# Weight decodes from buffers of their own, spread between the attention steps of a Nystrom attention and MoE kernel

## The chip, the cores and the metric

The kernel runs on one core of a Trainium2 chip. The metric is the device time of one execution in microseconds (us), taken as the median of several runs. The engines are PE (TensorE, matrix products), DVE (VectorE), ACT (ScalarE), POOL (GpSimd) and SP (SyncE, which issues most DMAs here).

## What is computed

The inputs are random q, k, v (4 batches, 8 heads, 576 positions, 64 wide, float32) and weights that arrive as float64.

```python
# attention, per batch and head (32 landmarks: means of 18 rows each)
A, Bm, C = sm(q, k_lm), sm(q_lm, k_lm), sm(q_lm, k)      # softmax of scaled products
Z = Bm.T / (norm1(Bm) * norminf(Bm) + 1e-6)
for _ in range(6):
    Z = 2 * Z - Z @ Bm @ Z
x = A @ Z @ C @ v                                        # then reshaped to (2304, 512)
# dense softplus network
x = softplus(x @ w_in) @ w_out                           # 512 -> 2048 -> 512
# top-1 experts: 8 experts, 512 -> 1024 -> 512
e = argmax(x @ w_gate)
out = softmax(x @ w_gate)[e] * sigmoid(x @ w_output_gate)[e] * (relu(x @ w1[e]) @ w2[e])
```

## The kernel before

Three stages follow one another: the attention (0 to 149 us of the profiled span), the dense network, and the routed experts. The change touches the attention stage and what is prepared in it for the dense network.

**Attention.** The 32 batch-head pairs are taken in 8 groups of 4 heads; two groups make a pair, one for each batch. A group goes through steps, each a function of the kernel, and a string PLAN names them by a letter and a number: K loads k and q of a group, V loads v, M makes the landmark means (L199, L207), T transposes k and q, C and A are the two score products with their softmax, N is the small landmark softmax and the six Newton steps of a pair (PE L292, DVE L296 and L297), E transposes C's result and multiplies it with v (L354), F finishes a pair: a product with Z (ps_w, L365), a masked copy on DVE (wbd, L370), eight products (ps_x, L380), copies on ACT (xo, L382) and stores to DRAM from ACT's queue (xT_d, L385). T has eight pieces a group; a piece is one product of constant ones (`warm`, L163, 128x512 in bf16, its result overwritten), three transposes (L187) and one ACT copy out of PSUM (L189).

**Preparing weights.** W0 to W7 each load 512 KB of the float64 w_in (`raw`, L392) and turn it into two float32 parts. `decode_f64` does: ACT absolute value (`deca`, L93), three DVE passes over 128x512 (L94, L96, L98), and a guard against tiny numbers, which here runs as two POOL instructions (L103, L104); elsewhere in the kernel the guard is one DVE instruction (L101). Then ACT writes the high part (`whi`, L109) and POOL the low part (`wlo`, L110). O does the same for 128 rows of w_out, X loads a first piece of the attention's result back from DRAM (`x0r`) and splits it. In the kernel before, `raw` and `x0r` take turns in the three-deep buffers of k, q and v.

**What sets the order.** PLAN's order is handed to a list scheduler, which gives earlier steps a higher priority and writes one fixed sequence for each engine; an engine runs its own sequence strictly in order. SP's DMA issues are in such a sequence too, and a load waits there until its buffer is free. The stages after the attention are in an order written by hand, which the change leaves alone. In the kernel before, SP first loads the two landmark constant columns (`lmc`), k0, q0, all other constants (`cst`, the 128-column identity first in it), k1, q1 and so on, and all W, O and X steps come behind F0.

**Behind the attention.** The dense network's first product is L621 (`ps_h`), its softplus starts at ACT L631 (`t`), and its second product is L660. Its later weights are decoded on ACT and DVE while it runs.

Of the kernel before, what the change touches and what calls it, by code (L numbers as in the profile page):

```python
# [10 lines left out]
F32 = DT.float32  # L11
F32R = DT.float32r
BF16 = DT.bfloat16
I32 = DT.int32
# [7 lines left out]
B, H, S, D = 4, 8, 576, 64  # L22
M = 32
NT, DM = B * S, H * D
FF = 2048
NE, F2 = 8, 1024
# [3 lines left out]
CH = 256  # L30
# [4 lines left out]
NC6 = S // TP  # L35
HALF = S // 2
NB = 1
PLAN = """
K1 T0 M0 M1 A0 C0 T1 K2 M2 C1 K3 V0 A1 K4 V1 T2 E0 C2 E1 T3 M3 N0 V2 K5 K6 V3 T4 A2 C3 A3 F0 V4 E2 M4 A4 M5 T5 K7 E3
N1 X0 V5 M6 C4 T6 C5 C6 E4 M7 V6 V7 N2 A5 E5 W0 F1 N3 W1 W2 E6 W3 T7 A6 W4 O0 C7 A7 W5 F2 W6 E7 W7 F3  # L40
"""
NWA = 8
JOINT = 3
# [40 lines left out]
CONST, COFF = const_table()  # L84


def decode_f64(nc, pool, src, shape, tag="dect", guard="vector", **kw):

    w = src.rearrange("p a (n two) -> p a n two", two=2)
    lo32, hi32 = w[:, :, :, 0], w[:, :, :, 1]  # L90
    t = pool.tile(shape, I32, tag=tag, name="dect", **kw)
    a = pool.tile(shape, F32, tag="deca", name="deca", **kw)
    nc.scalar.activation(a, hi32.bitcast(F32), AF.Abs)  # L93
    nc.vector.tensor_scalar(t, a.bitcast(I32), 3, 0x3FFFFFFF, ALU.logical_shift_left, ALU.bitwise_and)  # L94
    yield
    nc.vector.scalar_tensor_tensor(t, hi32, -0x40000000, t, ALU.bitwise_and, ALU.bitwise_or)  # L96
    yield
    nc.vector.scalar_tensor_tensor(t, lo32, 29, t, ALU.logical_shift_right, ALU.bitwise_or)  # L98
    yield
    if guard == "vector":  # L100
        nc.vector.scalar_tensor_tensor(a, a, 3.4332275390625e-05, t.bitcast(F32), ALU.is_ge, ALU.mult)  # L101
    else:
        nc.gpsimd.tensor_scalar(a, a, 3.4332275390625e-05, None, ALU.is_ge)  # L103
        nc.gpsimd.tensor_tensor(a, a, t.bitcast(F32), ALU.mult)  # L104
    yield a


def split_hi_lo(nc, a, dst_hi, dst_lo, lo_engine):
    nc.scalar.activation(dst_hi, a, AF.Copy)  # L109
    lo_engine.tensor_tensor(dst_lo, a, dst_hi.bitcast(F32), ALU.subtract)  # L110
# [8 lines left out]
def moe_nystrom_kernel(ctx: ExitStack, tc: tile.TileContext, q, k, v, w_in, w_out, w_gate, w_ogate, w1, w2,  # L119
                       consts, out):  # L120
    nc = tc.nc
# [8 lines left out]
    cst = cpool.tile([128, CONST.shape[1] - 98], F32, name="cst")  # L130
# [13 lines left out]


    with ExitStack() as actx:
        a1 = actx.enter_context(tc.tile_pool(name="a1", bufs=1))
        a2 = actx.enter_context(tc.tile_pool(name="a2", bufs=2))
        a3 = actx.enter_context(tc.tile_pool(name="a3", bufs=3))
        ld = actx.enter_context(tc.tile_pool(name="a_ld", bufs=3))  # L150
        pt = actx.enter_context(tc.tile_pool(name="pt", bufs=2, space=PSUM))
        pss = actx.enter_context(tc.tile_pool(name="pss", bufs=2, space=PSUM))
        psm = actx.enter_context(tc.tile_pool(name="psm", bufs=1, space=PSUM))
# [7 lines left out]
        def warm(ps):  # L161

            nc.tensor.matmul(ps, dense[:, :128], dense, start=True, stop=True)  # L163

        def load_qk(g):
            b, hg = divmod(g, 2)
            r = R[g] = {}
            for nm, src in (("k", k), ("q", q)):
                t = ld.tile([TP, 4, NC6 * D], F32, tag=nm, name=f"{nm}{g}")
                nc.sync.dma_start(t, src[b, 4 * hg:4 * hg + 4].rearrange("h (p c) d -> p h (c d)", c=NC6))  # L170
                r[nm] = t
# [8 lines left out]
        def transposes(r, g):  # L180
            for nm in ("k", "q"):
                xt = a2.tile([128, 4, HALF], F32, tag=nm + "T", name=nm + "T", bufs=3)
                for h in range(4):
                    ps = pt.tile([128, 512], F32, tag="pt", name="ps_t")
                    warm(ps)
                    for c in range(3):
                        nc.tensor.transpose(ps[:, c * TP:(c + 1) * TP], r[nm][:, h, c * 128:(c + 1) * 128],  # L187
                                            ident[:TP, :TP])
                    nc.scalar.activation(xt[:, h], ps[:, :HALF], AF.Copy)  # L189
                    yield  # L190
                r[nm + "T"] = xt
# [195 lines left out]

        def decode_w_in(i):
            n = FF // 16
            raw = ld.tile([128, NC6 * 4 * D], I32, tag="kqv"[i % 3], name="raw")  # L390
            raw = raw[:, :8 * n].rearrange("p (k f) -> p k f", k=4)
            nc.sync.dma_start(raw, w_in.bitcast(I32).rearrange("(k p) f -> p k f", p=128)[:, :, 2 * n * i:2 * n * (i + 1)])  # L392
            a = list(decode_f64(nc, a3, raw, [128, 4, n], bufs=2, guard="gpsimd"))[-1]
            split_hi_lo(nc, a, whi[0][:, :, i * n:(i + 1) * n], wlo[0][:, :, i * n:(i + 1) * n], nc.gpsimd)

        def run_all(gen):
# [6 lines left out]
            return [R[2 * b], R[2 * b + 1]]  # L403

        nc.scalar.preload_act_table_set("natural_log_exp_and_others")
        nc.sync.dma_start(lmc, consts[:, CONST.shape[1] - 98:])
        load_qk(0)
        nc.sync.dma_start(cst, consts[:, :CONST.shape[1] - 98])
        def prep_x0():
            xr = ld.tile([128, 4, CH], F32, tag="k", name="x0r")  # L410
            nc.sync.dma_start(xr, xT_d[0].rearrange("(k p) n -> p k n", p=128)[:, :, :CH])
            split_hi_lo(nc, xr, x0[0], x0[1], nc.gpsimd)

        def prep_wo0():
            raw = ld.tile([128, 2 * DM], I32, tag="q", name="raw")
            nc.sync.dma_start(raw, w_out.bitcast(I32)[:128, :])
            a = list(decode_f64(nc, a3, raw.unsqueeze(1), [128, 1, DM], bufs=2, guard="gpsimd"))[-1]
            split_hi_lo(nc, a[:, 0], wo0[0], wo0[1], nc.gpsimd)

        steps = {  # L420
# [9 lines left out]
            "X": lambda _: prep_x0(),  # L430
            "O": lambda _: prep_wo0(),
            "W": decode_w_in,
        }
        for step in PLAN.split():
# [33 lines left out]
    raw, xgs, xt, slot_pools = [], {}, {}, {}  # L468
# [78 lines left out]
    with ExitStack() as mctx:  # L547
# [42 lines left out]
        def load_xr(c):  # L590
            if c <= JOINT - 1:
                t = m2.tile([128, 4, CH], F32, tag="x2", name="xr", bufs=3)
                xr = [t[:, :2], t[:, 2:]]
            else:
                xr = [m2.tile([128, 2, CH], F32, tag="deca", name="xr") for _ in range(2)]
            t0 = c * CH
            while t0 < (c + 1) * CH:
                b, o = divmod(t0, S)
                n = min(S - o, (c + 1) * CH - t0)
                for j in range(2):  # L600
                    nc.sync.dma_start(xr[j][:, :, t0 - c * CH:t0 - c * CH + n],
                                      xT_d[b].rearrange("(k p) n -> p k n", p=128)[:, 2 * j:2 * j + 2, o:o + n])
                t0 += n
            return xr
# [238 lines left out]
        with tc.manual_schedule():  # L843
            xs = {0: x0}
            xr = [load_xr(c) for c in range(1, JOINT)]
# [33 lines left out]
            for i in range(len(order) + LAG):  # L879
# [14 lines left out]
                if i < len(order):  # L894
                    c, p = order[i]
                    if i == nj - 1:
                        xr.append(load_xr(JOINT))
                    h = gemm1(p, xs[c], *HB.get(i, ()))
# [190 lines left out]
```

## Time and profile before

| | |
|---|---|
| runs | 935.37, 937.71, 937.09 us; median 937.09 |
| profiled execution | 937.34 us, span 935.6 us |
| busy share of the span | PE 93%, PEld 77%, DVE 72%, ACT 63%, POOL 26% |
| mean granted clock of TensorE | 0.977 |
| the chain that ended last | PE 59%, DVE 19%, ACT 10% |
| attention stage | from 0 to 149.40 us, the first product of the dense network |

The share of the busy time is one over all stages. The rows further down are of three views. One gives the busy time of each engine in a stretch, with the granted clock of TensorE (1.00 is full speed) and the share that the DMA engines were busy. One is the list of instructions in order of time, with the idle time before each and what ended it. One groups instructions of a line and a shape.

### The profile page before, as it was taken

What the parts mean: (1) busy time and instruction counts of PE and PEld (TensorE: products, weight loads), DVE (VectorE), ACT (ScalarE), POOL (GpSimd) and SP (SyncE); (2) the same over time, 40 slices, a digit from 0 to 9 for tenths busy, and PEclk for the clock granted to TensorE, in tenths of its full rate; (3) what the DMA queues carried; (4) which work ended last, traced back from release to release, by engine and by line L of the source; (5) the groups of instructions that cost most, each with busy time, mean ns of one, the idle gap of its engine ahead of it and who ended that gap; (6) DMA issues with size and microseconds to landing.
All of it is one profiled execution on the core that took longest, in us unless ns stands there. A gap on an engine that the chain in (4) does not pass through costs nothing.

```text
span 935.6 us, 15483 instructions
## 1 busy us (share of the span) xinstructions
PE 868.9 (93%) x5826; PEld 723.2 (77%) x5826; DVE 677.1 (72%) x1146; ACT 589.9 (63%) x958; POOL 239.0 (26%) x125
## 2 busy tenths in 40 slices
PE   5998987888888999999999999998999999999996
PEld 3666645677677899999899998887778888878885
DVE  0847696787887546455645555667899999899994
ACT  2554555555565565555655555464888888988883
POOL 0001384000000000000000000014566767666762
PEclk9999998898988999999999999999999999999998
DMA  9856545122221100010110100050116649541610
GB/s 218 200 130 175 158 147 169 68 90 74 84 91 35 31 3 24 1 46 24 46 46 1 46 1 23 24 203 24 57 34 216 225 142 360 198 154 35 209 43 32
DMA packets 49516, 90.93 MB, mean 97 GB/s; under 512 B 5471, under 2 KB 32095, under 8 KB 47392
## 3 DMA queue, kind: packets, MB, share of 16 engines
q1 hardware_dynamic: 41408, 74.43, 25.5%
q0 software_dynamic: 3680, 10.78, 3.5%
q10 hardware_dynamic: 4352, 4.72, 1.5%
q8 instruction: 47, 0.77, 0.3%
q14 instruction: 29, 0.24, 0.1%
HBM read 134.46 MB, written 15.48 MB: 160 GB/s over the span
## 4 chain that ended last, share of the span: by engine, by line
PE 59%; DVE 19%; ACT 10%; issue 6%; DMA 4%; POOL 2%; SPq 0%; POOLq 0%; ACTq 0%; DVEq 0%
PE ps_h L621 16%; PE acc L660 13%; PE ps_g L958 9%; PE ps_y L984 8%; DVE lo L481 2%; DVE dect L96 2%; DVE dect L98 2%; ACT hi L479 2%; DMA raw<-in_moe_w 2%; PE ps_lg L685 2%; DVE gl L650 2%; ACT gh L649 1%; PE ps_hT L972 1%; DVE deca L101 1%; PE ps_t L187 1%
## 5 line engine op out<-in xcount | busy, mean ns | idle before, releaser
L481 DVE TENSOR_TENSOR lo<-raw,hi 128x1024 fp32r<-128x1024 f32 x129 | 225.3, 1774 | 11.7 <-ACT hi L479 11.5
L479 ACT ACTIVATE hi<-raw 128x1024 fp32r<-128x1024 f32 x176 | 176.9, 1063 | 10.0 <-DMA raw<-in_moe_w 9.2
L621 PE MATMUL ps_h<-xh,whi 128*128 128x256 f32 x512 | 149.6, 292 | 14.1 <-DVE d L642 12.4
L488 POOL DMA_INDIRECT xg<-x_d,gidx x23 | 37.9, 1648 | 463.9 <-ACT t L631 452.9
L621 PE MATMUL ps_h<-xl,whi 128*128 128x256 f32 x512 | 147.0, 287 | 0.3 <-DVE xl L110 0.3
L621 PE MATMUL ps_h<-xh,wlo 128*128 128x256 f32 x512 | 146.9, 287 | 0.0
L650 DVE TENSOR_TENSOR gl<-l,gh 128x512 fp32r<-128x512 f32 x72 | 49.8, 692 | 123.2 <-ACT gh L649 122.2
L481 POOL TENSOR_TENSOR lo<-raw,hi 128x1024 fp32r<-128x1024 f32 x47 | 118.0, 2512 | 38.4 <-ACT hi L479 38.3
L621 PEld LDWEIGHTS ps_h<-xh,whi 128*128 128x128 f32 x512 | 100.0, 195 | 19.7 <-DVE d L642 16.1
L621 PEld LDWEIGHTS ps_h<-xl,whi 128*128 128x128 f32 x512 | 100.2, 196 | 1.9 <-DVE xl L110 0.5
L621 PEld LDWEIGHTS ps_h<-xh,wlo 128*128 128x128 f32 x512 | 100.1, 196 | 0.0
L660 PE MATMUL acc<-woh,gh 128*128 128x512 f32 x240 | 97.0, 404 | 2.9 <-ACT woh L109 2.9
L660 PE MATMUL acc<-wol,gh 128*128 128x512 f32 x240 | 95.3, 397 | 1.0 <-DVE wol L110 1.0
L660 PE MATMUL acc<-woh,gl 128*128 128x512 f32 x240 | 94.3, 393 | 0.0
L631 ACT ACTIVATE t<-ps_h 128x512 f32<-128x512 f32 x72 | 42.6, 592 | 67.9 <-PE ps_h L621 47.9
L635 ACT ACTIVATE l<-t 128x512 f32<-128x512 f32 x72 | 45.5, 632 | 55.1 <-DVE gl L650 55.1
L984 PE MATMUL ps_y<-hi,hh 128*128 128x512 f32 x184 | 76.7, 417 | 0.2 <-ACT hh L976 0.2
L984 PE MATMUL ps_y<-hi,hlo 128*128 128x512 f32 x184 | 73.4, 399 | 1.7 <-DVE hlo L977 1.6
L958 PE MATMUL ps_g<-hi,x0l 128*128 128x512 f32 x184 | 73.6, 400 | 0.2
L984 PE MATMUL ps_y<-lo,hh 128*128 128x512 f32 x184 | 72.7, 395 | 0.0
L958 PE MATMUL ps_g<-hi,x0h 128*128 128x512 f32 x184 | 72.0, 392 | 0.0
L958 PE MATMUL ps_g<-lo,x0h 128*128 128x512 f32 x184 | 72.0, 391 | 0.0
(266 smaller groups left out, 1838.8 us busy)
## 6 DMA issues: line engine op xcount, KB each, us to landing
raw<-in_moe_w SPq DMA_DIRECT2D x88, 1024.0 KB
raw<-in_moe_w_in SPq DMA_DIRECT2D x16, 512.0 KB
raw<-in_moe_w_out SPq DMA_DIRECT2D x16, 512.0 KB
x_d<-x SPq DMA_DIRECT2D x9, 514.0 KB
k<-in_k SPq DMA_DIRECT2D x8, 576.0 KB
q<-in_q SPq DMA_DIRECT2D x8, 576.0 KB
v<-in_v SPq DMA_DIRECT2D x8, 576.0 KB
xT_d<-xo ACTq DMA_DIRECT2D x16, 288.0 KB
```

The lines of the kernel that those rows point to most:

```text
L96: nc.vector.scalar_tensor_tensor(t, hi32, -0x40000000, t, ALU.bitwise_and, ALU.bitwise_or)
L98: nc.vector.scalar_tensor_tensor(t, lo32, 29, t, ALU.logical_shift_right, ALU.bitwise_or)
L479: nc.scalar.activation(w[0][:, us], raw[i][:, us], AF.Copy)
L481: eng.tensor_tensor(w[1][:, us], raw[i][:, us], w[0][:, us].bitcast(F32), ALU.subtract)
L488: nc.gpsimd.indirect_dma_start(out=xg, out_offset=None, in_=src, in_offset=bass.IndirectOffsetOnAxis(ap=gidx[:, s:s + 1], axis=0))
L621: nc.tensor.matmul(ps[:, i], a[:, kk], b_[:, kk], start=n == 0, stop=n == 11)
L631: nc.scalar.activation(t, h, AF.Abs)
L635: nc.scalar.activation(l, t, AF.Ln, bias=1.0)
L650: nc.vector.tensor_tensor(gl, l, gh.bitcast(F32), ALU.subtract)
L660: nc.tensor.matmul(acc[tt], a[:, i, ts_], b_[f], start=f == 0 and n == 0, stop=f == NFF - 1 and n == 2)
L958: nc.tensor.matmul(ps, a[:, kk], b_[:, kk], start=n == 0, stop=n == 11)
L984: nc.tensor.matmul(y, a[:, kk], b_[:, kk], start=half == 0 and n == 0, stop=half == 1 and n == 11)
```

## The change

1. **PLAN is a new order.** Landmarks come before transposes, and the W steps come early and between the attention steps. A line and a half of it stand in the diff; the pieces below show what the engines then run.
2. **Own buffers.** w_in, w_out and x0r are loaded into two buffers of their own (tag "raw"); load n+2 waits until decode n has read its buffer. The loads' pool is opened first.
3. **Guard on VectorE.** The nine decodes of the stage use the one DVE instruction (L101) in place of the two on POOL.
4. **Fewer constant products in T.** The product of ones runs for the first of four heads only: 2 a group in place of 8, 48 fewer in all.
5. **Start.** 18 products of ones run before anything is loaded; the identity is loaded first, then `lmc`, k0, q0, k1, q1 and then the other constants.

```diff
-K1 T0 M0 M1 A0 C0 T1 K2 M2 C1 K3 V0 A1 K4 V1 T2 E0 C2 E1 T3 M3 N0 V2 K5 K6 V3 T4 A2 C3 A3 F0 V4 E2 M4 A4 M5 T5 K7 E3
+M0 M1 K2 T0 V0 C0 A0 M2 T1 E0 A1 V1 C1 T2 K3 C2 M3 K4 K5 T3 E1 V2 K6 M4 T4 V3 W0 W1 C3 A2 N0 F0 T5 N1 A3 V4 A4 W2 E2
...
-                    warm(ps)
+                    if h == 0:
+                        warm(ps)
...
-            raw = ld.tile([128, NC6 * 4 * D], I32, tag="kqv"[i % 3], name="raw")
-            raw = raw[:, :8 * n].rearrange("p (k f) -> p k f", k=4)
+            raw = ld.tile([128, 8 * n], I32, tag="raw", name="raw", bufs=2).rearrange("p (k f) -> p k f", k=4)
...
-            a = list(decode_f64(nc, a3, raw, [128, 4, n], bufs=2, guard="gpsimd"))[-1]
+            a = list(decode_f64(nc, a3, raw, [128, 4, n], bufs=2))[-1]
...
+        ps0 = psm.tile([128, 512], F32, tag="sm0", name="ps_0")
+        for _ in range(18):
+            warm(ps0)
+        nc.sync.dma_start(cst[:, :128], consts[:, :128])
         nc.sync.dma_start(lmc, consts[:, CONST.shape[1] - 98:])
         load_qk(0)
-        nc.sync.dma_start(cst, consts[:, :CONST.shape[1] - 98])
+        load_qk(1)
+        nc.sync.dma_start(cst[:, 128:], consts[:, 128:CONST.shape[1] - 98])
...
-            xr = ld.tile([128, 4, CH], F32, tag="k", name="x0r")
+            xr = ld.tile([128, 4, CH], F32, tag="raw", name="x0r", bufs=2)
...
-            raw = ld.tile([128, 2 * DM], I32, tag="q", name="raw")
+            raw = ld.tile([128, 2 * DM], I32, tag="raw", name="raw", bufs=2)
...
-            a = list(decode_f64(nc, a3, raw.unsqueeze(1), [128, 1, DM], bufs=2, guard="gpsimd"))[-1]
+            a = list(decode_f64(nc, a3, raw.unsqueeze(1), [128, 1, DM], bufs=2))[-1]
```

SP's sequence becomes: identity, lmc, k0, q0, k1, q1, the other constants, k2, q2, v0, v1, v2, raw of W0 and W1, k3, q3, and from there a raw load between every one to four of the other loads; x0r stands after q7, and raw of W7, v5, v6 and v7 behind it.

**ACT, from the copy of the landmark sums of the third group on** (`l_...` is that copy, `lm` the landmarks, `kT` and `qT` T's copies out of PSUM). Before:

```order
L312 ACTIVATE ec,rc<-ps_c,nb 128x576
L203 ACTIVATE l_322<-ps_l_309 128x256
L210 ACTIVATE lm<-ps_lm 128x256
L189 ACTIVATE kT<-ps_t 128x288
L327 ACTIVATE asm<-asm 128x576
L189 ACTIVATE kT<-ps_t 128x288 x3
L189 ACTIVATE qT<-ps_t 128x288 x4
```

After:

```order
L313 ACTIVATE ec,rc<-ps_c,nb 128x576
L204 ACTIVATE l_288<-ps_l_275 128x256
L93 ACTIVATE deca<-raw 128x512 x2
L211 ACTIVATE lm<-ps_lm 128x256
L190 ACTIVATE kT<-ps_t 128x288 x4
L190 ACTIVATE qT<-ps_t 128x288
L328 ACTIVATE asm<-asm 128x576
L190 ACTIVATE qT<-ps_t 128x288
L109 ACTIVATE whi_72<-deca 128x4x128
```

The first instructions of the decodes W0 and W1, which wait for their loads, now stand ahead of the third group's landmarks and T1's copies; before, no decode stands near.

**DVE, around the first Newton steps of the first pair** (`n_...` and `ry` belong to N, `asm`, `amx` to A). Before:

```order
L271 TENSOR_TENSOR ry<-bme,n_638 128x2x32
L272 TENSOR_SCALAR n_638<-n_638 128x2
L323 STREAM_TRANSPOSE asm<-ps_a 128x576
L274 SCALAR_TENSOR_TENSOR ry<-ps_r,n_638,cst 128x128 x2
L325 TENSOR_REDUCE amx<-asm 128x18
L326 TENSOR_TENSOR asm<-asm,amx 128x576
L296 COPY ry<-ps_u 128x2x128
L297 TENSOR_TENSOR ry<-ry,ps_u 128x2x32
```

After:

```order
L275 SCALAR_TENSOR_TENSOR ry<-ps_r,n_778,cst 128x128 x2
L94 TENSOR_SCALAR dect<-deca 128x512
L324 STREAM_TRANSPOSE asm<-ps_a 128x576
L96 SCALAR_TENSOR_TENSOR dect<-raw,dect 128x512
L326 TENSOR_REDUCE amx<-asm 128x18
L94 TENSOR_SCALAR dect<-deca 128x512
L98 SCALAR_TENSOR_TENSOR dect<-raw,dect 128x512
L297 COPY ry<-ps_u 128x2x128
L298 TENSOR_TENSOR ry<-ry,ps_u 128x2x32
L327 TENSOR_TENSOR asm<-asm,amx 128x576
L96 SCALAR_TENSOR_TENSOR dect<-raw,dect 128x512
L101 SCALAR_TENSOR_TENSOR deca<-deca,dect 128x512
```

Passes of W0 and W1 now stand between N0's Newton steps and the softmax of A. Seven of the eight W decodes and O stand in this way ahead of F0's products, where before none did.

**ACT, the end of the stage** (`xr` is a piece of the attention's result that is loaded back, `t` the first instruction of the softplus). Before:

```order
L382 ACTIVATE xo<-ps_x 128x576
L109 ACTIVATE xh<-xr 128x512
L385 DMA xT_d<-xo 128x2x288
L109 ACTIVATE whi_72<-deca 128x4x128
L109 ACTIVATE xh<-xr 128x512
L382 ACTIVATE xo<-ps_x 128x576
L385 DMA xT_d<-xo 128x2x288
L631 ACTIVATE t<-ps_h 128x512
```

After:

```order
L383 ACTIVATE xo<-ps_x 128x576
L386 DMA xT_d<-xo 128x2x288
L383 ACTIVATE xo<-ps_x 128x576
L386 DMA xT_d<-xo 128x2x288
L383 ACTIVATE xo<-ps_x 128x576
L386 DMA xT_d<-xo 128x2x288
L636 ACTIVATE t<-ps_h 128x512
```

The last decode's `whi` and two `xh` are gone from between the last copies of F3; W7's `whi` now stands some forty instructions earlier.

## Rows read from the trace of the kernel before

**Rows 1.** Stretches: length, busy (count) PE, PEld, DVE, ACT, POOL; clock, DMA share, GB/s

```profile
0.00:8.70 8.70, 1.89 (x4) 0.43 (x4) 0.48 (x1) 1.28 (x1) 0.19 (x4) 1.00 0.78 179
0.00:30.40 30.40, 19.93 (x230) 12.38 (x234) 8.56 (x27) 10.99 (x26) 0.19 (x4) 1.00 1.02 223
```

**Rows 2.** DMA issues of the first 100 us: names, queue, count, KB each

```profile
k<-in_k SPq DMA_DIRECT2D x8, 576.0 KB
...
raw<-in_moe_w_in SPq DMA_DIRECT2D x5, 512.0 KB
```

**Rows 3.** PE in time: start, length, line, names, count, idle before and its end

```profile
11.05 0.71 PE L187 MATMUL ps_t<-cst,k 96*128 96x96 f32 x3 [7.71 <-DMA cst<-in_consts]
```

**Rows 4.** One stretch, DVE alone: busy (count), clock, DMA share, GB/s

```profile
20.00:61.50 41.50, 27.77 (x81) 1.00 0.76 180
```

**Rows 5.** DVE groups by shape, 157 to 300 us: busy us, mean ns, idle before

```profile
L98 DVE SCALAR_TENSOR_TENSOR dect<-raw,dect 128x512 int32<-128x512 int32 x23 | 15.9, 690 | 0.6
L96 DVE SCALAR_TENSOR_TENSOR dect<-raw,dect 128x512 int32<-128x512 int32 x23 | 15.9, 690 | 0.5
L101 DVE SCALAR_TENSOR_TENSOR deca<-deca,dect 128x512 f32<-128x512 f32 x22 | 15.2, 690 | 0.5
...
L94 DVE TENSOR_SCALAR dect<-deca 128x512 int32<-128x512 int32 x23 | 9.7, 421 | 3.0 <-ACT deca L93 3.0
```

**Rows 6.** PE in time: F0's first products, and the first of the dense network

```profile
61.97 1.24 PE L380 MATMUL ps_x<-at,wbd 64*128 64x288 f32 x8
...
149.40 0.39 PE L621 MATMUL ps_h<-x0h,whi 128*128 128x256 f32 x1
```

**Rows 7.** Stretches from F0 on, columns as in Rows 1

```profile
62.00:149.40 87.40, 75.41 (x944) 47.53 (x943) 65.97 (x177) 46.89 (x100) 39.79 (x27) 0.96 0.55 160
125.00:139.00 14.00, 12.38 (x142) 6.99 (x140) 14.00 (x30) 9.31 (x19) 11.58 (x8) 1.00 0.44 140
139.00:149.40 10.40, 6.02 (x24) 2.86 (x24) 8.28 (x15) 5.08 (x9) 7.52 (x6) 0.67 0.61 186
```

**Rows 8.** PE in time: two pieces of T at full clock

```profile
120.88 0.38 PE L163 MATMUL ps_t<-dense 128*128 128x512 bf16 x1
121.10 0.41 PE L187 MATMUL ps_t<-cst,k 96*128 96x96 f32 x3
121.35 0.38 PE L163 MATMUL ps_t<-dense 128*128 128x512 bf16 x1
```

**Rows 9.** PE in time: the last pair's F

```profile
140.18 0.43 PE L365 MATMUL ps_w<-cv,zbd 128*128 128x64 f32 x2 [1.49 <-DVE zbd L281]
...
144.20 2.29 PE L380 MATMUL ps_x<-at,wbd 64*128 64x288 f32 x8 [3.21 <-DVE wbd L370]
```

**Rows 10.** The chain that ended last: the two products of one landmark step

```profile
18.92 0.69 PE ps_lm L207 x16
19.60 1.43 PE ps_l L199 x24
```

**Rows 11.** ACT in time: the wait for x0r, and the start of the softplus

```profile
82.71 1.06 ACT L109 ACTIVATE x0h<-x0r 128x1024 fp32r<-128x1024 f32 x1 [1.65 <-DMA x0r<-xT_d]
...
152.60 0.63 ACT L109 ACTIVATE whi<-deca 128x512 fp32r<-128x512 f32 x1 [3.09 <-POOL deca L104]
...
154.74 0.60 ACT L631 ACTIVATE t<-ps_h 128x512 f32<-128x512 f32 x1 [0.44 <-ACT xo L382]
```

**Rows 12.** PE in time: end of the first ps_h, first second product

```profile
152.25 0.28 PE L621 MATMUL ps_h<-x0h,wlo 128*128 128x256 f32 x1
...
161.72 0.50 PE L660 MATMUL acc<-wo0h,gh 128*128 128x512 f32 x1 [3.43 <-ACT gh L649]
```

**Rows 13.** POOL and DVE in time, side by side, near 140 us

```profile
139.94 1.31 POOL L104 TENSOR_TENSOR deca<-deca,dect 128x512 f32<-128x512 f32 x1 [1.08 <-DVE dect L98]
...
140.05 1.75 DVE L98 SCALAR_TENSOR_TENSOR dect<-raw,dect 128x512 int32<-128x512 int32 x1
```

**Rows 14.** POOL groups by shape, 75 to 150 us: busy us, mean ns

```profile
L103 POOL TENSOR_SCALAR deca<-deca 128x512 f32<-128x512 f32 x9 | 15.5, 1734 | 22.1 <-DVE dect L94 22.1
L104 POOL TENSOR_TENSOR deca<-deca,dect 128x512 f32<-128x512 f32 x9 | 14.3, 1594 | 3.6 <-DVE dect L98 2.9 <-DVE amx L330 0.7
```

More of the change, by code (lines that the diff above doesn't have):

```diff
@@ L38 @@
 PLAN = """
-K1 T0 M0 M1 A0 C0 T1 K2 M2 C1 K3 V0 A1 K4 V1 T2 E0 C2 E1 T3 M3 N0 V2 K5 K6 V3 T4 A2 C3 A3 F0 V4 E2 M4 A4 M5 T5 K7 E3
-N1 X0 V5 M6 C4 T6 C5 C6 E4 M7 V6 V7 N2 A5 E5 W0 F1 N3 W1 W2 E6 W3 T7 A6 W4 O0 C7 A7 W5 F2 W6 E7 W7 F3
+M0 M1 K2 T0 V0 C0 A0 M2 T1 E0 A1 V1 C1 T2 K3 C2 M3 K4 K5 T3 E1 V2 K6 M4 T4 V3 W0 W1 C3 A2 N0 F0 T5 N1 A3 V4 A4 W2 E2
+V5 M5 W3 E3 K7 M6 C4 C5 T6 C6 E4 A5 N2 M7 W4 V6 F1 V7 T7 N3 C7 E5 E6 A6 A7 E7 O0 F2 W5 W6 X0 F3 W7
 """
@@ L146, in moe_nystrom_kernel @@
     with ExitStack() as actx:
+        ld = actx.enter_context(tc.tile_pool(name="a_ld", bufs=3))
         a1 = actx.enter_context(tc.tile_pool(name="a1", bufs=1))
@@ L149, in moe_nystrom_kernel @@
         a3 = actx.enter_context(tc.tile_pool(name="a3", bufs=3))
-        ld = actx.enter_context(tc.tile_pool(name="a_ld", bufs=3))
         pt = actx.enter_context(tc.tile_pool(name="pt", bufs=2, space=PSUM))
```

## The prediction

> **What bounds the kernel now.** The page gives PE 93% of the whole span, but the change works in the attention, so I read stretches of that stage first. From F0's first products to the dense network's first product, 61.97 to 149.40 us [rows 6], PE is busy 75.41 of 87.40 us [rows 7]: 12.0 us of idle time are all that a better order can win there, apart from PE work that goes away. DVE is busy 65.97 us of it, and 14.00 of 14.00 us from 125 to 139 us, where the decodes stand among the softmax [rows 7]. So PE bounds that stretch as a whole, DVE its end. In the 10.4 us before the dense network the granted clock is 0.67 and PE is busy only 6.02 us [rows 7]: it waits 1.49 us and 3.21 us for DVE, and F3's eight products take 2.29 us where F0's took 1.24 [rows 9, 6]. Before F0 no decode is made, and DVE is busy 27.77 of 41.50 us [rows 4]: room that the change fills. Then I read the list of ACT around the softplus, since ACT runs in order: it stood 3.09 us waiting for POOL's guard at 152.60 and started `t` at 154.74 [rows 11]. The sum is made against the profiled execution, 937.34 us, 0.25 above the median of 937.09. About 0.3% (2.8 us) is what a measurement of this kernel can tell from no change.
>
> **Part 1: the loads gate the early decodes.** Ahead of W1's data SP's queue holds 0.45 MB of constants, nine loads of 576 KB (0.590 MB each) and two of 512 KB (0.524 MB) [rows 2]: 6.8 MB. Before, 223 GB/s moved 6.8 MB by 30.4 us [rows 1]; W0's data are 6.3 MB in, by 28.2 us. Moved is not yet usable: 1.6 MB (lmc, k0, q0, cst) were moved by about 8.7 us at 179 GB/s [rows 1], while the first transposes got their constants at 11.05 [rows 3], 2.3 us later. So W0's data are usable near 30.6 and W1's near 32.7. ACT's sequence has both absolute values ahead of the third group's landmarks and T1's copies, so ACT, and PE behind its PSUM tiles, stand for some microseconds until 33; before, no such wait exists. It costs PE time that PE had to spare before F0, so it is paid in the next part. With 0.67 for the absolute value DVE begins W0 at 31.3. The first pieces of group 0 gain: the identity no longer comes behind k0 and q0, but landmarks need k0, q0 as before. The 18 products at the start end long before k0 is there; I cost them, and the other pool order, at nothing: PE then waits 7.71 us for loads anyway [rows 3], so even 18 at half clock lie under that wait.
>
> **Part 2: DVE paces up to F0.** Before, 27.77 us in 81 instructions, 0.343 each, made the scores and the Newton steps up to F0 [rows 4]. About 16 of them stand ahead of W0's first pass in the new sequence, 5.5 us; 22.3 us are left. Eight decodes (seven W and O) now stand ahead of F0's products. One costs DVE 0.42 for L94 and three times 0.69, the guard L101 among them: 2.49 us [rows 5]; eight are 19.9 us. Together 42.2 us from 31.3. With DVE always busy, as in 125 to 139 us, F0 comes at 73.5; busy at 80%, 8.28 of 10.40 as in the last stretch [rows 7], at 84.0. I take 95%, nearer to the first, since there too decodes fill the holes that softmax steps leave: **F0 at 75.7**, 13.7 us later than before. That loss buys eight of nine decodes, of which none were done at this point before.
>
> **Part 3: PE from F0 on.** It has the same groups to finish, less what goes away: of its 75.4 us busy
> - 18 products of ones in T5 to T7 go (six a group). One takes 0.22 us from its start to that of the transposes behind it [rows 8]: 4.0.
> - One landmark step more stands ahead of F0: 1.43 and 0.69 [rows 10], 2.1.
> - The lower clock near the end goes if PE no longer waits there: about 4.4 of the 6.02 us [rows 7] lie at the lower level (F3's 2.29 against 1.24 [rows 9, 6]), half of that, 2.2.
>
> That leaves 67.1, or 142.8 us with no wait at all. **Waits:** before 12.0. Gone is what the decodes made: DVE has one decode in place of nine after F0, so 20 us of its 65.97 [rows 7, 5], and the 3.21 for `wbd` [rows 9] loses its cause. What stays is the end of each pair's Newton chain, which a step more or less of DVE does not shorten: 1.49 [rows 9] for three pairs, 4.5. X0 still waits for F0's result on ACT, 1.65 before [rows 11], with two of T's copies queued behind it on ACT and PE behind those; I take it as lying inside. Bounds: 3 (two chains) and 12 (as before). First dense product **147.3**, 2.1 earlier than 149.40.
>
> **Part 4: the start of the softplus.** The first `ps_h` was done just after the row at 152.25 [rows 12], `t` began at 154.74, since ACT ran `whi` late behind the guard [rows 11]. In the new sequence the copies of F3 are followed by `t` alone. That is 2.2 us less what one copy still takes beyond the products: **2.0**, out of the 3.43 that PE waited before the second product [rows 12]. If that wait came from the later steps of the softplus instead, it is 0.
>
> **Part 5: the guard.** On DVE it costs 0.69 for each of nine [rows 5], counted in part 2. On POOL it took 1.73 and 1.59 [rows 14], up to 3.3 us of latency in each decode; no separate gain but the one in part 4. DVE's passes also ran long beside it: L98 took 1.75 at 140.05 while POOL's L104 ran from 139.94 [rows 13], against 0.69 [rows 5]. I add nothing for this, as only that one row shows it so plainly; at one microsecond for each of half the nine it would be 4 more, which the low end holds in part.
>
> The Trainium skill ("SBUF — State Buffer", section "SBUF: two separate sides") says that a GpSimd instruction and a DVE one with two SBUF inputs lock a shared port pair for a whole instruction each. The row at 140.05 agrees with it; by the rule every two-input pass under POOL's work would stretch and the sum would be several microseconds lower, up to the 4 just named.
>
> **The sum.** −2.1 and −2.0: −4.1 on 937.34, **933.2 us**.
>
> **Rivals.**
> *Even (gain taken back).* F3's Newton chain, softmax and wait for `wbd` all sit at the end of the plan whatever the decodes do. If the 3.21 [rows 9] stays, the total is 936.4. For it: the last four F steps always end on DVE. Against it: the row just ahead of that wait is a decode's L98, 1.75 long [rows 13].
> *Slower: loads that ACT and SP wait for in order.* Two buffers for raw mean that load n+2 waits for decode n, and all of SP's later loads wait behind it; on ACT each absolute value waits for its load, with T's copies behind it. If that empties DVE to 80%, F0 comes at 84.0: +8.3 −4.1, **941.5**. It decides when F0's first product comes after about 79.8. For it: ACT waited for x0r 1.65 in order [rows 11]. Against: DMA carried 180 GB/s of the 223 it can [rows 4, 1], so the bytes fit.
> *Even: the clock.* Before, every piece of T has its product of ones, and in 125 to 139 us the clock is 1.00 [rows 7]. With one piece in four the granted clock may fall to the lower of its two levels (1.2 in place of 2.4 GHz) during T; a lapse as at the end costs 2.2 us (part 3). Two lapses: 937.6. No row shows transposes without these products.
>
> The Trainium skill ("TensorE: Matmul & The Clock Gate", section "Part 4: PE-mode transpose") speaks against this part of the change: transposes do not count as busy work for the full clock. No row here can show it; by that rule the two lapses come, and the time is the one just named.
>
> *The start does nothing.* Had the 18 products and the identity no effect at all, the sum would stay, since it counts them at nothing.
>
> **How the numbers follow.** Forecast 0.50, its own range 927 to 934.5: F0 at 73.5 and waits of 3 give 929.5, and 2.5 less for part 5. Gain taken back 0.20, the clock 0.12: both within 0.3%, 0.32 together. Slower 0.18, at 941.5, or with waits of 12 at 940.7. The range of 8 in 10 goes from 927 to 941.5: it holds all cases at their own time and leaves out the ends. Faster 0.50, same 0.32, slower 0.18.
>
> **What would show it.** Right: W0's first DVE pass near 31, F0's `ps_x` near 75.7, DVE over 90% busy from 31 to 75, first dense product near 147, `t` right behind the first `ps_h`. Wrong: F0 past 80; idle PE time over 8 us between F0 and the dense network; the clock below 1.00 in T's stretches; PE's wait before the second product still over 3 us. What I trust least is the 95%: each point of it moves F0 by 0.5 us.

## The result, and the profile after

The changed kernel takes 948.16 us (median of 4 runs, 946.37 to 950.17) against 936.82 for the kernel before: 1.0118 times, 95% interval 1.0096 to 1.0140. It is **slower by 11.3 us** where 4.1 us less was forecast. The profiled execution took 949.34 us, span 947.5.

The new lines that answer to rows 3 and 6, PE in time (start, length, line, names, count, idle before and its end): F0's first products, the first product of the dense network, and its second product.

```profile
78.72 1.24 PE L381 MATMUL ps_x<-at,wbd 64*128 64x288 f32 x8 [0.24 <-DVE wbd L371]
...
161.00 0.58 PE L626 MATMUL ps_h<-x0h,whi 128*128 128x256 f32 x1 [0.75 <-ACT xo L383]
...
173.39 0.50 PE L665 MATMUL acc<-wo0h,gh 128*128 128x512 f32 x1 [1.30 <-ACT gh L654]
```

F0 is 16.8 us later than in [rows 6], the dense network starts 11.6 us later, and its second product 11.7 us later than in [rows 12]. So 11.7 of the 12.0 us between the two profiled executions arise up to the dense network's second product. Between F0 and the dense network it is 82.3 us in place of 87.4: 5.1 of the 16.8 us come back, where the forecast wanted all of them and more. The stretches that answer to [rows 7], the whole one and three pieces of it (length, busy and count of PE, PEld, DVE, ACT, POOL, then granted clock, DMA share, GB/s):

```profile
78.70:161.00 82.30, 73.79 (x887) 45.32 (x887) 52.96 (x154) 39.15 (x87) 4.96 (x3) 0.91 0.42 127
92.00:110.00 18.00, 15.93 (x229) 9.53 (x228) 11.68 (x34) 9.16 (x21) 3.63 (x2) 0.72 0.17 44
110.00:146.00 36.00, 35.72 (x495) 24.47 (x491) 28.69 (x90) 17.78 (x42) 0.00 (x0) 1.00 0.35 107
146.40:161.00 14.60, 10.12 (x50) 4.49 (x46) 4.11 (x12) 7.46 (x13) 0.00 (x0) 0.82 0.67 209
```

PE has 57 instructions fewer than in [rows 7] and DVE 13 us less to do, but PE's busy time fell by 1.6 us only: the granted clock is 0.91 in place of 0.96. It is low from 92 to 110 us and from 146.4 to 161, and 1.00 in between, where T's pieces near 111 to 116 and 123 to 134 us ran with one product of ones in four pieces. ACT in time tells where the waits are:

```profile
30.82 0.66 ACT L93 ACTIVATE deca<-raw 128x512 f32<-128x512 f32 x1 [5.08 <-DMA raw<-in_moe_w_in]
33.13 0.66 ACT L93 ACTIVATE deca<-raw 128x512 f32<-128x512 f32 x1 [1.65 <-DMA raw<-in_moe_w_in]
...
47.70 0.66 ACT L93 ACTIVATE deca<-raw 128x512 f32<-128x512 f32 x1 [3.26 <-DMA raw<-in_moe_w_in]
...
92.18 1.06 ACT L109 ACTIVATE x0h<-x0r 128x1024 fp32r<-128x1024 f32 x1 [4.32 <-DMA x0r<-xT_d]
...
154.77 0.65 ACT L383 ACTIVATE xo<-ps_x 128x576 f32<-128x576 f32 x1 [1.89 <-DMA xT_d<-xo]
...
157.71 0.65 ACT L383 ACTIVATE xo<-ps_x 128x576 f32<-128x576 f32 x1 [2.28 <-DMA xT_d<-xo]
158.85 0.65 ACT L383 ACTIVATE xo<-ps_x 128x576 f32<-128x576 f32 x1 [0.50 <-DMA xT_d<-xo]
...
166.38 0.60 ACT L636 ACTIVATE t<-ps_h 128x512 f32<-128x512 f32 x1 [5.43 <-PE ps_h L626]
```

The decodes ahead of F0 stand waiting for their loads, x0r costs 4.32 us instead of 1.65 [rows 11], and at the end there is something that the kernel before does not have in this form: copies out of PSUM (`xo`) wait for their own stores to DRAM. There are three xo buffers. F2's and F3's first `ps_x` lay 12 us apart before and lie 4.5 us apart now, so eight copies come in a row; from the fourth on each needs a buffer that an earlier copy of the row has filled, and the fifth to the seventh waited for its store. PE stands behind ACT in both low stretches:

```profile
93.59 0.38 PE L163 MATMUL ps_et<-dense 128*128 128x512 bf16 x1 [2.79 <-ACT qT L190]
...
155.48 0.38 PE L163 MATMUL ps_x<-dense 128*128 128x512 bf16 x1 [1.48 <-ACT xo L383]
...
158.41 0.58 PE L163 MATMUL ps_x<-dense 128*128 128x512 bf16 x1 [1.29 <-ACT xo L383]
```

The `qT` of the first is the copy right behind `x0h`, the one that waits for x0r. The chain that ended last shows the price of the stores (start, length, what):

```profile
151.19 0.55 ACT xo L383
151.76 5.86 DMA xT_d<-xo
...
157.71 0.66 ACT xo L383
...
158.41 0.58 PE ps_x L163
158.99 1.29 PE ps_x L381 x4
160.30 0.66 ACT xo L383
...
161.00 5.35 PE ps_h L626 x24
```

A store of 5.86 us stands on the chain, and behind it the products run at the lower clock: the last four `ps_x` take 1.29 us (eight of F0's take 1.24), and the first 24 products of the dense network 5.35, where before the first `ps_h` took about 3 us from 149.40 [rows 6, 12].

### The profile page after: what moved, and what is told of

It is laid out like the page before. It is cut to its first block, busy times and chain, and to the rows that moved or that the text cites. A ratio compares the mean times of both kernels' runs of the same rounds, so it can differ in the third digit from the quotient of the medians.

```text
span 947.5 us, 15444 instructions
## 1 busy us (share of the span) xinstructions
PE 874.2 (92%) x5796; PEld 723.4 (76%) x5796; DVE 681.9 (72%) x1155; ACT 588.4 (62%) x958; POOL 208.9 (22%) x107
## 4 chain that ended last, share of the span: by engine, by line
PE 62%; DVE 15%; ACT 9%; DMA 7%; issue 5%; SPq 1%; POOL 0%; ACTq 0%; POOLq 0%; DVEq 0%
PE ps_h L626 17%; PE acc L665 13%; PE ps_g L963 10%; PE ps_y L989 9%; DMA raw<-in_moe_w_in 3%; DMA raw<-in_moe_w 2%; DVE lo L486 2%; PE ps_hT L977 2%; PE ps_lg L690 1%; DVE deca L101 1%; DVE dect L96 1%; ACT hi L484 1%; DVE dect L98 1%; ACT gh L654 1%; DVE gl L655 1%
```

## Experiments

Each kernel is the changed one or the one before with one part undone or done alone. Each ratio and its 95% interval are against the kernel before on the same chip (medians 936.8 to 937.3 us). A single interval reaches 0.1 to 0.4% to either side, so a difference between two experiments of less than about 3 us (0.3%) is not read as shown. A trace is one execution and can lie several us off the median.

**The PLAN of before, all else changed** (`e1_oldplan`).

```diff
-M0 M1 K2 T0 V0 C0 A0 M2 T1 E0 ...
+T0 M0 M1 A0 C0 T1 K2 M2 C1 K3 ...
```

> The changed kernel with the PLAN of before; own buffers, guard on VectorE, the start and the sparse products of ones stay. Theory A (the order costs: early decodes hold ACT and so PE, x0r and the two last F steps stand late): F0's first product near 62 to 66 us, first dense product at 149 to 153 us, total 934 to 940 us. Theory B (the clock costs, since most transposes have no product of ones beside them): the old order has just as few of them, so the clock lapses stay, total 943 us or more.

932.76 us, 0.9958 (0.9943 to 0.9972): **faster than both**. F0's first product came at 56.63, the dense network at 141.06. The new PLAN is what costs, 15.4 us; the other four parts together gain 4.5. Theory B alone cannot explain the slowdown, as these transposes have as few products of ones; in its trace the clock was 1.00 from 11 us up to F0.

**Products of ones in every piece of T again** (`e2_warmall`).

```diff
-                    if h == 0:
-                        warm(ps)
+                    warm(ps)
```

> The changed kernel with a product of ones in every piece of T again (48 more, 0.22 us each at full clock). Theory B (clock): granted clock 0.98 or more from 16 to 146 us, first dense product 4 to 7 us earlier than 161.0, total 941 to 944 us. Theory A (order): the clock is lost in waits for ACT, not for want of these products; the total is 948 to 953 us, as PE has up to 10 us more to do.

950.78 us, 1.0136 (1.0119 to 1.0153): not faster than the changed kernel; the 2.6 us more are within the noise. From F0 on (81.28 us) the clock was 0.98 and PE busy 71.84 us in place of 73.79, although 18 of the 48 products stand there, but F0 came 2.6 us later, and the dense network still began at 160.91. These products are no way out here.

**Six xo buffers** (`e3_xobufs`). The sequences of all engines are those of the changed kernel, but for the place of one store.

```diff
-                    xo = a3.tile([128, 2, HALF], F32, tag="xo", name="xo")
+                    xo = a3.tile([128, 2, HALF], F32, tag="xo", name="xo", bufs=6)
```

> The changed kernel with six xo buffers in place of three; PE's and DVE's order are untouched. Theory C (the last eight copies out of F2 and F3 wait for their own stores to DRAM, 1.9 and 2.3 us in the trace): these waits go, the first dense product comes 3 to 6 us earlier (the lower clock that follows the waits goes too), total 943 to 945.5 us. Against it: the dense network is late by its other inputs, total 947 to 949 us.

940.84 us, 1.0043 (1.0026 to 1.0060): 7.3 us less than the changed kernel, more than expected. The last copies, ACT in time:

```profile
147.29 0.65 ACT L383 ACTIVATE xo<-ps_x 128x576 f32<-128x576 f32 x1 [0.44 <-PE ps_x L381]
...
148.62 0.65 ACT L383 ACTIVATE xo<-ps_x 128x576 f32<-128x576 f32 x1 [0.68 <-PE ps_x L381]
...
149.77 0.65 ACT L383 ACTIVATE xo<-ps_x 128x576 f32<-128x576 f32 x1 [0.50 <-ACT xo L383]
```

None waits for a store: here the eight copies start within 8.1 us (141.72 to 149.77), in the changed kernel within 11.9. From F2's first `ps_x` (140.92) to the dense network (150.47) it is 9.6 us; in the changed kernel 13.4 (147.56 to 161.00). That is 3.9 us of the gain. The first 24 products, now at full clock, are 2.2 more: from the first to the second product of the dense network it is 10.2 us (150.47 to 160.67) in place of 12.4. In its profile F0 also came 3.8 us earlier (74.88), with raw loads that landed 2 us sooner; the order ahead of F0 is the same, and a single execution cannot tell whether this is more than scatter.

**Guard on POOL again** (`e4_guardpool`).

```diff
-            a = list(decode_f64(nc, a3, raw, [128, 4, n], bufs=2))[-1]
+            a = list(decode_f64(nc, a3, raw, [128, 4, n], bufs=2, guard="gpsimd"))[-1]
```

> The changed kernel with the guard on POOL again (two instructions for each of nine decodes). Theory D (the guard's 6.2 us on DVE delay F0): F0 3 to 6 us earlier than 78.7, total 943 to 946 us. Theory A: POOL's 3.3 us of latency and its hold on DVE's two-input passes cost as much or more; F0 at 78 to 84 us, total 948 to 954 us.

952.03 us, 1.0155 (1.0129 to 1.0181), F0 at 82.68. The guard's 6.2 us on DVE are not the cause: on POOL it is 3.9 us worse in this order (the two intervals just overlap).

**X0, W0 and W1 directly behind F0** (`e5_x0first`). x0r then takes the first raw buffer, and no decode runs ahead of F0.

```diff
-... T4 V3 W0 W1 C3 A2 N0 F0 T5 N1 ... O0 F2 W5 W6 X0 F3 W7
+... T4 V3 C3 A2 N0 F0 X0 W0 W1 T5 N1 ... O0 F2 W5 W6 F3 W7
```

> The changed kernel with three letters of its PLAN moved: X0, W0 and W1 stand directly behind F0 (X0 takes the first raw buffer, so no decode comes ahead of F0); the order of the attention steps stays. Theory A1 (the decodes ahead of F0 are what the new order costs, through ACT's waits for their loads and DVE's passes): F0's first product near 58 to 64 us, total 938 to 942 us. Theory A2 (the new order of the attention steps costs by itself, F2 and F3 bunched at the end): F0 comes early but the dense network still starts at 157 us or later, total 945 to 948 us.

944.52 us, 1.0079 (1.0053 to 1.0105): 3.6 us less than the changed kernel, between the two theories; the intervals of the two kernels overlap. PE in time, and the stretch ahead of F0 (columns as above):

```profile
67.67 1.24 PE L381 MATMUL ps_x<-at,wbd 64*128 64x288 f32 x8
...
153.62 0.58 PE L626 MATMUL ps_h<-x0h,whi 128*128 128x256 f32 x1 [0.75 <-ACT xo L383]
```

```profile
31.00:66.00 35.00, 33.33 (x461) 23.78 (x457) 25.02 (x75) 20.24 (x52) 0.00 (x0) 1.00 0.57 151
```

F0 is 11.1 us earlier in this trace, though not at the 58 to 64 us of theory A1: with no decode ahead of F0, PE is busy 33.33 of 35.00 us at full clock, so PE's work on the attention steps of the new PLAN alone holds F0 near 67 us. The stretch behind F0 is 85.95 us: 3.7 of the 11.1 us are given back. (This execution took 940.92 us, 3.6 less than the median.) The copies again wait for stores, 2.46, 1.44 and 0.50 us.

**The high part of x0r by POOL** (`e6_x0pool`).

```diff
-            split_hi_lo(nc, xr, x0[0], x0[1], nc.gpsimd)
+            nc.gpsimd.tensor_copy(x0[0], xr)
+            nc.gpsimd.tensor_tensor(x0[1], xr, x0[0].bitcast(F32), ALU.subtract)
```

> The changed kernel with the high part of x0r made by POOL, so that ACT does not stand 4.3 us for that load in order. If that wait costs: PE's wait of 2.8 us near 93 us and the lower clock behind it go, total 943 to 946 us. If the time is set by what comes later: 947 to 950 us.

950.32 us, 1.0129 (1.0099 to 1.0160). ACT's wait for x0r, the longest behind F0, is gone and nothing is gained: other waits take its place, among them 4.08 us for a raw load at 98.67 and the same stores at the end.

**Both: X0, W0, W1 behind F0 and six xo buffers** (`e8_x0first_xo6`). It differs from `e5_x0first` in the xo buffers only.

```diff
+                    xo = a3.tile([128, 2, HALF], F32, tag="xo", name="xo", bufs=6)
...
+... T4 V3 C3 A2 N0 F0 X0 W0 W1 T5 N1 ...
```

> X0, W0 and W1 behind F0 and six xo buffers, all else as in the changed kernel. If the early decodes and the wait of the last copies for their stores are two separate costs, both gains add: 931 to 936 us. If they are one and the same (a bunched end that only has to be reached later), it gives no more than either: 938 to 942 us.

936.27 us, 0.9993 (0.9975 to 1.0011): the slowdown is gone, 11.9 us. The two add: 8.3 us by the buffers on top of 3.6; taken the other way round, 4.6 us by the moved steps on top of the 7.3 of `e3_xobufs`. This is the cleanest evidence for the stores, since nothing else changed between the two kernels.

**Six xo buffers in the old order** (`e7_old_xo6`).

```diff
-M0 M1 K2 T0 V0 C0 A0 M2 T1 E0 ...
+T0 M0 M1 A0 C0 T1 K2 M2 C1 K3 ...
...
+                    xo = a3.tile([128, 2, HALF], F32, tag="xo", name="xo", bufs=6)
```

> The PLAN of before with all other parts of the change, and six xo buffers. In its trace with three buffers one copy waited 1.74 us for a store near 143 us. If the stores hold F3 only where F2 and F3 are bunched: within 1 us of 932.8. If stores hold it in every order: 929 to 931 us.

932.68 us, 0.9947 (0.9926 to 0.9967), the same as `e1_oldplan`. Where F2 and F3 lie apart, three buffers do; the one wait of 1.74 us costs nothing that the medians show. This kernel and `e1_oldplan` have nearly the same sequences, and yet their profiled executions differ early on. The stretches of `e1_oldplan`, columns as above:

```profile
11.00:24.00 13.00, 11.02 (x178) 6.81 (x178) 6.68 (x18) 6.62 (x20) 0.00 (x0) 1.00 1.09 260
...
36.00:50.00 14.00, 13.14 (x226) 9.04 (x226) 6.75 (x19) 7.50 (x19) 0.00 (x0) 1.00 0.66 165
50.00:62.00 12.00, 10.82 (x135) 6.87 (x125) 9.19 (x33) 6.77 (x16) 0.00 (x0) 1.00 0.43 114
```

And of `e7_old_xo6`:

```profile
11.00:24.00 13.00, 10.92 (x169) 6.39 (x168) 6.20 (x17) 5.86 (x16) 0.00 (x0) 0.89 1.09 246
...
36.00:50.00 14.00, 12.59 (x177) 8.80 (x166) 7.17 (x18) 6.47 (x16) 0.00 (x0) 0.82 0.87 186
50.00:62.00 12.00, 11.07 (x111) 6.77 (x100) 5.06 (x16) 5.08 (x14) 0.00 (x0) 0.64 0.42 100
```

With the clock at 1.00 F0 came at 56.63, with lapses at 63.37. So with few products of ones the clock lapsed in one of these executions and not in the other. Whether this is what scatters the times is not shown: with a product in every piece the next kernel scatters no less.

**Old order, products in every piece of T** (`e9_old_warmall`).

```diff
-M0 M1 K2 T0 V0 C0 A0 M2 T1 E0 ...
+T0 M0 M1 A0 C0 T1 K2 M2 C1 K3 ...
...
-                    if h == 0:
-                        warm(ps)
+                    warm(ps)
```

> PLAN of before, own buffers, guard on VectorE and the new start, with a product of ones in every piece of T again. Two runs of this order with the sparse products had F0's first product at 56.6 us with a granted clock of 1.00 and at 63.4 us with lapses to 0.64 to 0.89. Theory B (sparse products let the clock lapse, which costs the old order too): clock 0.99 or more from 11 to 62 us, F0 at 56 to 59 us, total 928 to 931 us, and runs that lie closer together. Rival: the 48 products cost as much as the clock gives back: 932 to 935 us.

936.01 us, 0.9987 (0.9972 to 1.0003): 3.3 us more than with the sparse products, and its runs lie no closer together (932.52 to 939.00, against 930.02 to 935.15 of `e1_oldplan`). The clock was 1.00 up to 62 us and F0 came at 58.20, as theory B said, but later stretches had lapses too (0.83 to 0.87 from 62 to 120 us), and the total follows the rival. In this order, with the new start, fewer products are a gain in spite of the lapses.

**Old order and old start** (`e10_old_start`).

```diff
-M0 M1 K2 T0 V0 C0 A0 M2 T1 E0 ...
+T0 M0 M1 A0 C0 T1 K2 M2 C1 K3 ...
...
-        for _ in range(18):
-            warm(ps0)
-        nc.sync.dma_start(cst[:, :128], consts[:, :128])
...
-        load_qk(1)
-        nc.sync.dma_start(cst[:, 128:], consts[:, 128:CONST.shape[1] - 98])
+        nc.sync.dma_start(cst, consts[:, :CONST.shape[1] - 98])
+        load_qk(1)
```

> PLAN and start of before (no 18 products, loads in the old order), own buffers, guard on VectorE, sparse products of ones. If the new start is what the 4.5 us come from: 936 to 938 us. If it gives little or nothing: 931 to 934 us.

943.45 us, 1.0059 (1.0041 to 1.0078): the new start is worth **10.7 us** here, which I had costed at nothing. PE in time, transposes of the first and the second group and F0:

```profile
10.19 2.44 PE L188 MATMUL ps_t<-cst,k 96*128 96x96 f32 x12 [7.26 <-DMA cst<-in_consts]
...
24.91 0.41 PE L188 MATMUL ps_t<-cst,k 96*128 96x96 f32 x3
...
32.68 0.74 PE L188 MATMUL ps_t<-cst,q 96*128 96x96 f32 x3
33.59 0.69 PE L188 MATMUL ps_t<-cst,q 96*128 96x96 f32 x3
...
69.56 1.24 PE L381 MATMUL ps_x<-at,wbd 64*128 64x288 f32 x8
```

In `e1_oldplan`, with the new start, the first transposes come at 8.08, and six take 0.66 us, there and again at 32.68:

```profile
8.08 0.66 PE L188 MATMUL ps_t<-cst,k 96*128 96x96 f32 x6
...
32.68 0.66 PE L188 MATMUL ps_t<-cst,q 96*128 96x96 f32 x6
```

So without the new start PE begins 2.1 us later and at the lower level, reaches the higher one (0.41 for three at 24.91), and has lost it again at 32.68. (The clock column of the stretches reads 1.00 from 11 to 24 us here; the lengths of the products contradict it.) No run parts the 18 products from the new order of the loads.

**The guard on VectorE alone** (`e11_guard`), in the kernel before.

```diff
-            a = list(decode_f64(nc, a3, raw, [128, 4, n], bufs=2, guard="gpsimd"))[-1]
+            a = list(decode_f64(nc, a3, raw, [128, 4, n], bufs=2))[-1]
```

> The kernel before with the guard of the nine decodes on VectorE alone. If the guard's move is the gain that the old order shows (no wait of 3.1 us for POOL ahead of the softplus, no DVE passes stretched beside POOL): 932 to 935 us. If it only moves 6 us of work to an engine that was busy all of 125 to 139 us: 937 to 940 us.

938.56 us, 1.0023 (1.0013 to 1.0032). PE's wait before the second product fell to 1.24 from 3.43 [rows 12], as part 4 said, but DVE was busy 20.00 of 20.00 us from 120 to 140: no gain by itself, and 0.2% slower.

**The new PLAN alone** (`e12_planonly`), in the kernel before.

```diff
-K1 T0 M0 M1 A0 C0 T1 K2 M2 C1 ...
+K1 M0 M1 K2 T0 V0 C0 A0 M2 T1 ...
```

> The kernel before with the new PLAN alone: buffers of k, q and v for the raw loads, guard on POOL, all products of ones, old start. No decode comes ahead of F0 in its order but the first absolute value. Theory A2 (the new order of the attention steps costs by itself, 7 to 11 us): 944 to 950 us. Theory A1' (it costs only together with the own buffers, which let the decodes run ahead of F0): 936 to 941 us.

939.88 us, 1.0037 (1.0023 to 1.0052). PE in time:

```profile
70.72 1.24 PE L380 MATMUL ps_x<-at,wbd 64*128 64x288 f32 x8
...
156.31 0.38 PE L621 MATMUL ps_h<-x0h,whi 128*128 128x256 f32 x1 [1.06 <-ACT xo L382]
```

F0 is 8.8 us later with no decode ahead of it but an absolute value and one DVE pass: the attention steps of the new PLAN do this by themselves. At the end eight copies come in a row here too, spread over 10.1 us (145.50 to 155.60) with the decodes' work between them, and none waits for a store. The PLAN costs 2.6 us only.

**Own buffers undone** (`e13_kqv`), all else changed.

```diff
-            raw = ld.tile([128, 8 * n], I32, tag="raw", name="raw", bufs=2).rearrange("p (k f) -> p k f", k=4)
+            raw = ld.tile([128, NC6 * 4 * D], I32, tag="kqv"[i % 3], name="raw")
...
-            xr = ld.tile([128, 4, CH], F32, tag="raw", name="x0r", bufs=2)
+            xr = ld.tile([128, 4, CH], F32, tag="k", name="x0r")
```

> The changed kernel with raw and x0r in the buffers of k, q and v, as before; PLAN, guard, sparse products and start as in the change. If the own buffers are what makes the new PLAN dear, by letting the decodes and their waits ahead of F0: F0's first product at 64 to 71 us, total 940 to 945 us. If the PLAN costs the same either way: 946 to 950 us.

947.70 us, 1.0109 (1.0073 to 1.0145), the same as the changed kernel: the theory that the own buffers make the PLAN dear **fell**. Beside `e15_start_sparse` below, which has the old PLAN, the old buffers and the guard on POOL, the new PLAN costs 14.3 us. PE in time:

```profile
65.83 1.24 PE L381 MATMUL ps_x<-at,wbd 64*128 64x288 f32 x8
...
157.69 0.58 PE L627 MATMUL ps_h<-x0h,whi 128*128 128x256 f32 x1 [5.91 <-ACT xo L383]
```

F0 came 12.9 us earlier than in the changed kernel, as expected, and the stretch behind it grew by 9.6 to 91.9 us. One copy waited 3.71 us for a store at 154.37, PE 5.91 us for the last copies, and the clock was 0.74 from 100 to 120 us.

**The new start alone** (`e14_start`) and **with the sparse products** (`e15_start_sparse`), in the kernel before.

```diff
+        for _ in range(18):
+            warm(ps0)
+        nc.sync.dma_start(cst[:, :128], consts[:, :128])
...
+        load_qk(1)
+        nc.sync.dma_start(cst[:, 128:], consts[:, 128:CONST.shape[1] - 98])
```

```diff
-                    warm(ps)
+                    if h == 0:
+                        warm(ps)
```

> The kernel before with the new start alone (18 products of ones, identity first, k1 and q1 ahead of the other constants). If PE's idle first 11 us are worth time by themselves: F0 3 to 6 us earlier than 61.97, total 930 to 934 us. If the start only helps where T has few products of ones: 936 to 938 us.

> The kernel before with the new start and the sparse products of ones; buffers, guard and PLAN of before. If these two are the whole gain that the old order shows: 930 to 934 us. If own buffers and guard bring a part of it: 935 to 938 us.

936.08 us, 0.9983 (0.9969 to 0.9996), and 933.44 us, 0.9960 (0.9945 to 0.9975). In the first F0 came 3.9 us earlier (58.06), yet F3's products still waited 3.21 us for `wbd`, as in [rows 9], and came only 1.6 us earlier (142.61). The second cannot be told from the whole gain of the old order (`e1_oldplan`), so own buffers and guard add nothing that is shown. Start and sparse products belong together: the start alone brings 0.2%, and the sparse products without it stand in `e10_old_start`, 6.2 us slower than the kernel before; with own buffers and guard as before they were not run.

## Why the prediction was wrong, point by point

- **Part 1, the loads: right.** W0's absolute value began at 30.82 (30.6 forecast) and W1's at 33.13 (32.7), and ACT stood 5.08 and 1.65 us for them. PE stood too: until 32.69, for 4.09 us, for DVE's pass over A's scores, which comes behind W0's first pass in DVE's sequence, and until 34.12, for 1.03, for ACT's `lm`.
- **Part 2, F0: near in number, right in part, with luck.** F0 came 3.0 us late. DVE in 31 to 75 us:

```profile
31.00:75.00 44.00, 39.76 (x86) 0.88 0.72 195
```

It was busy 90.4%, not 95%: at 0.5 us a point, 2.3 of the 3.0. The point from which the slower rival was to decide, 79.8, was not reached, so that rival, as it was put, is not what happened. But the sum has DVE as the only pace ahead of F0, and takes PE to have time to spare there. By its own rows F0 would come at 54.8 without any decode (22.3 us of DVE at 95%, from 31.3). `e5_x0first` and `e8_x0first_xo6`, which have no decode there, measured 67.67 and 66.58, with PE busy 33.33 and 33.26 of the 35.00 us from 31 to 66. So the decodes moved F0 by 11 to 12 us, not by the 20.9 that the sum has for them, and that 75.7 came so near is in part luck.
- **Part 3, from F0 on: the step that failed.** 82.3 us in place of 71.6. Two terms of the sum made this: PE's work, 73.79 us where 67.1 were forecast, and its waits, 8.5 where 4.5 were.
- **PE's work: the clock term had the wrong sign.** I had taken 2.2 us off for a clock that would no longer lapse; instead it went from 0.96 to 0.91. As an estimate from these means, 0.09 of 82.3 us at half the clock's level is 14.8 us at the lower level and 7.4 us of PE's time, against 3.5 before: 3.9 more, and with the 2.2 taken off 6.1 of the 6.7. `e2_warmall` agrees: with the clock at 0.98, PE's 71.84 us less 18 products of 0.22 are 67.9, near the 67.1. What is left of the 6.7 fits the step A3, which the sum overlooked: it stood ahead of F0 before and stands behind it now (80 products `ps_a` in place of 64). DVE had 13.0 us less to do behind F0, not 20: the guard had not been on DVE before, A3's passes came on, and so did four `xl` that had stood behind the dense network's first product. The clock rival named the lapses, but at 2.2 us each for two of them, and during T. They came where PE had stood behind ACT, and T's pieces between 110 and 146 us ran at 1.00.
- **The waits: the wrong ones.** The waits for `wbd` and `zbd` did go: F3's products waited for neither, and the only one left is 0.24 us at F0, so the *even* rival fell, and so did the 4.5 us that I had for three Newton chains. In their place came PE's wait of 2.79 us behind x0r, which I had taken as lying inside, and 1.48, 1.29 and 0.75 us behind copies held up by stores, 3.5 together. The new sequence of ACT that I had before me ends in copies and stores in a row, and I took that as a gain for the softplus; I never asked how many buffers xo has. More buffers were worth 7.3 to 8.3 us (`e3_xobufs`, `e8_x0first_xo6`), the largest single cause.
- **Part 4, the softplus: right, and taken back.** `t` followed the first `ps_h` and PE's wait before the second product fell from 3.43 to 1.30. But `ps_h` ran 2.2 us longer at the lower clock after the waits for stores, so from the first to the second product it is 12.4 us, as before (12.3). Where no copy waits for a store it is 10.2 (`e3_xobufs`) and 10.1 (`e8_x0first_xo6`), so the forecast 2.0 are there.
- **Part 5, the guard: right to give it no gain.** Alone it costs 0.2% (`e11_guard`); in the new order POOL is worse by 3.9 us. A DVE pass of two inputs stretched beside POOL's work in the changed kernel too, to 1.49 us at 43.74 beside a `wlo` that ran from 43.40 to 44.68, as in [rows 13], but that was no lever for the total.
- **The start: wrongly costed at nothing.** I asked only whether the 18 products lie under a wait, not at which clock the products behind them run, though the rows had it: the first three transposes took 0.71 us [rows 3], later ones 0.41 [rows 8]. The whole new start is worth 10.7 us where T has few products of ones, 0.2% in the kernel before.

The account of the miss: the profiled execution took 16.1 us more than the sum. 3.0 are F0, 10.7 the stretch behind it, 2.1 the gain of part 4 that was taken back, and 0.3 come later.

The account of the change: the four other parts −4.5 (`e1_oldplan`); the PLAN +15.4, of which 3.6 for X0 and the decodes ahead of F0, 8.3 for the stores at the end, and 3.5 for the order of the attention steps (`e8_x0first_xo6` against `e1_oldplan`). The stores are shown by undoing them, in two pairs of kernels; the 3.6 is at the edge of the noise, with 4.6 in the other pair; the last is a remainder. The decodes were expected to be the whole of it and were a quarter: where F0 comes 11.1 or 12.9 us earlier (`e5_x0first`, `e13_kqv`), 3.7 and 9.6 us are lost again behind it in the traces, and the medians gain 3.6 and 0.5.

Open is why the PLAN costs 2.6 us in the kernel before (`e12_planonly`) and 15.4 beside the other four parts. The products of ones do not decide it: with one in every piece it still costs 14.8 (`e2_warmall` against `e9_old_warmall`). Neither do the own buffers: 14.3 without them (`e13_kqv` against `e15_start_sparse`, which differ in the guard too). Left untested are the new PLAN with the old start in the changed kernel, and combinations.

The best kernel of the study is the old PLAN with the other four parts, 932.7 us in two kernels (0.9958 and 0.9947); the old kernel with the new start and sparse products only, 933.4, cannot be told from it.

## What to carry to other kernels

When a new order brings output steps together, count the buffers of the tile that they copy into and the time of one store: here three buffers and a store of 5.86 us held up eight copies that come in a row, whatever became earlier before. The pace counts too: `e12_planonly` had eight copies in a row, more spread out, and no wait. Before work is moved ahead of a stage, check whether the engine that paces what stands there has time to spare, and whether what follows runs without new waits; read the end of the new sequence as closely as the part that was improved. And do not cost products that only keep PE busy by the wait that hides them: look at the clock of the instructions behind them.

## What was not expected of the hardware

Nearly the same sequences gave a granted clock of 1.00 from 11 to 62 us in one profiled execution and as little as 0.64 in a stretch of another (`e1_oldplan`, `e7_old_xo6`), 6.7 us apart at F0. The Trainium skill ("TensorE: Matmul & The Clock Gate", section "Part 4: PE-mode transpose") says that transposes do not count as busy work for the full clock. These runs agree in part: in the old order with the new start, and one product of ones in four pieces, the clock fell below 1.00 between 11 and 62 us in two profiled executions of three (`e7_old_xo6`, `e15_start_sparse`); with one in every piece it stayed at 1.00 there in both of two (`e9_old_warmall`, `e14_start`). But `e1_oldplan` stayed there with one in four as well, and with the new start the extra products did not pay (`e2_warmall`, `e9_old_warmall`). With the old start they may: the one kernel with few products and the old start is the slow `e10_old_start`.
